# The last 64 columns of w_out loaded after the experts and unpacked as a ninth unit

## The chip, the cores and the metric

The kernel runs on one core of a Trainium2 chip. The metric is the device time of one execution in microseconds (us); shorter is better. A profiled execution also gives a trace, whose times count from the start of its span.

## The reference

Three layers run one after the other on 4608 tokens of 512 values:

```python
p_packed = sm_attn(p, k, v)              # attention into 32 packed rows, then back out
x = sm_attn(q, p_packed, p_packed)       # (batch 8, heads 8, 576, 64) -> (4608, 512)

logits = x @ phi                         # soft mixture of 8 experts, 4 slots each
slot_out[e] = relu(slot_input[e] @ w1[e]) @ w2[e]
x = softmax(logits, 1) @ slot_out

h = x @ w_in                             # 512 -> 1024
solu = h * softmax(h)
ln = (solu - mean) / sqrt(var + 1e-6) * g_ln
out = ln @ w_out                         # 1024 -> 512
```

[...]

## The kernel before

It has three phases. Phase 1 does the attention and the slots, unit by unit. Phase 2 streams the experts' weights (`w`, 29 loads of up to nine granules of 128x256) through TensorE, where a product per expert or block ends in `SO`. Then `sw` = `SO` x `wif` (the unpacked w_in) is summed over four pieces c for two halves n; the last, `sw(3, n)`, needs the last block's `SO`. `mk_sw` evicts each half on ACT and DVE into `swr`. Phase 3 makes 36 tiles of 128 tokens: `h` = cT x `swr` (`h_pe`), its negated row maximum (`nm`, `m_dve`), the exponential, `s3t`, the statistics on Pool, `hi` and `lo`, and the output matmuls `o` against `whi` and `wlo`, the two 16-bit halves of w_out.

All loads go out on SP's queue in the order of the list `order`, and land in 14 ring slots of 9216 bytes a partition (plus four in `ring2`). w_out is four loads of two chunks of 128x512 each, put in front of `("w", 4)` (`WO_AT`). They stay in their slots until the two halves have been made.

A w_out chunk is unpacked so (`mk_unpack`): DVE takes the exponent bits (`ux`, L1212) and the top mantissa word (`ua`, L1215), ACT scales the exponent by a Relu into bf16 bits (L1222), DVE adds the low word and the sign (L1227, L1234), and Pool multiplies both into the chunk (L1287). `wo_bound` lets TensorE add up |g| x exponents over all eight chunks into the bank `bd` (L1277). When all eight are in, ACT copies the bank to `winv` and DVE makes from it a power of two per column, `wsc`, and its inverse (L1296 to L1314). Then each chunk is scaled on DVE (`q1`, L1324), rounded on Pool to `whi` (`q2`, L1329), and the rest goes to `wlo` (`q3`, L1332).

The order of the work on each engine is fixed when the kernel is built. `Plan.op(engine, ns, function, deps, acq, rel, ...)` lists the operations with assumed durations, `LAT` holds assumed delays between engines, and `simulate` runs an engine's readiest and most urgent operation first: an engine that is free takes whatever is ready, and of several the one with the greatest `way` (longest way to the end, plus `urgent`). A random search with a fixed seed then shifts priorities and keeps what shortens the goals; phases 1 and 2 share one plan, phase 3 has its own, and all of the first plan stands ahead of the second on every engine. An engine executes in that order and waits wherever an input is late. Phase 3's tiles (`ep`, `tp`, `s3`) are laid over the ring's memory; one that lies over a ring slot waits until that slot's tile is released.

Of the kernel before, what the change touches and what calls it, by code (L numbers as in the profile page):

```python
# [185 lines left out]
def pack_attention__soft_moe__solu_kernel(  # L186
# [43 lines left out]
    WO_AT = 4  # L230
    NS1, NS2, NS3 = 122, 125, 142
# [21 lines left out]
    with ExitStack() as p12, tc.manual_schedule():  # L253
# [90 lines left out]
        for key in order:  # L344
# [13 lines left out]
            else:  # L358
                ns = 2540 if key[0] in ("wo", "wi") else 2850
# [835 lines left out]
        def mk_unpack(key, c, tail, deps, between=None):  # L1195
            def words():
                raw = loaded[key][:, 1024 * c:1024 * c + 1024].bitcast(UINT32).rearrange("p (n w) -> p n w", w=2)
                return raw[:, :, 0], raw[:, :, 1]

            def top():  # L1200
                raw = loaded[key][:, 1024 * c:1024 * c + 1024].bitcast(UINT16).rearrange("p (n w) -> p n w", w=4)
                return raw[:, :, 3]

            def dve():
# [3 lines left out]
                else:  # L1208
                    a = W["k"].tile([128, 512], FP32, tag="ua", name="ua")
                ua_t[key, c] = a  # L1210
                x = ux_t[key, c] = uk.tile([128, 512], UINT16, tag="ux", name="ux")
# [27 lines left out]
            ns = (1130, 670, 610, 740) if so else (1100, 720, 740, 1000)  # L1239
# [17 lines left out]
        def wo_chunk(k):  # L1257
            return loaded["wo", k // 2][:, 1024 * (k % 2):1024 * (k % 2) + 512]
# [14 lines left out]
        def wo_bound(k, key, c, dep):  # L1273
            def pe():
                if k == 0:
                    ps_t["bd"] = bank2()
                nc.tensor.matmul(  # L1277
                    out=ps_t["bd"], lhsT=W["ga"][:, k, :], rhs=ux_t[key, c].bitcast(BF16), start=(k == 0), stop=(k == 7)
                )

# [14 lines left out]
        def sc_act():  # L1295
            nc.scalar.copy(W["inv"], ps_t.pop("bd"))  # L1296

        def sc_dve():
            b = W["inv"].bitcast(UINT32)
            nc.vector.tensor_scalar(out=b, in0=b, scalar1=0x7F800000, scalar2=None, op0=ALU.bitwise_and)  # L1300

        def sc_dve2():
            W["sc"] = W["k"].tile([128, 512], FP32, tag="ua", name="wsc")
            nc.vector.tensor_scalar(
                out=W["sc"], in0=W["inv"].bitcast(UINT32), scalar1=24.0 * 2.0 ** 23, scalar2=None, op0=ALU.max
            )
# [476 lines left out]
```

## Time and profile before

| | us |
|---|---|
| median of three runs | 399.04 (398.42 to 399.07) |
| profiled execution | 398.32 |
| its span | 396.5 |

The profile shows for each engine when it worked and what ended its waits: PE is TensorE's matmul (PEld its weight loads), DVE VectorE, ACT ScalarE, POOL GpSimd, SP the queue that issues the loads. Busy time is given for the span and for stretches of it; the chain of waits goes back from the last instruction to what released each step. A wait for several things is put down to the one that came last.

### The profile page before, as it was taken

The page shows a single profiled execution, that of the slowest core. Times are in us where ns is not written, and L with a number is a line of the kernel's source. Part 1 is how long each engine was busy: PE and PEld are TensorE (multiplying, and loading weights), DVE is VectorE, ACT ScalarE, POOL GpSimd, SP SyncE. Part 2 cuts the span into 40 slices and gives each one's busy share as a digit, 9 for nine tenths or more (in the row PEclk, how much of TensorE's full clock was granted, in tenths as well). Part 3 has the DMA queues.
Part 4 walks back from the last instruction along what each step waited for, and adds up shares of the span by engine and source line. Part 5 has one row for each costly group of instructions (what it writes and reads, how often), then busy time and mean ns, then how long its engine had stood idle before and what let it go on. Part 6 is the DMA issues. An engine that isn't in the chain of part 4 may idle for free.

```text
span 396.5 us, 9563 instructions
## 1 busy us (share of the span) xinstructions
PE 375.6 (95%) x3760; PEld 198.0 (50%) x3760; DVE 285.4 (72%) x563; ACT 232.6 (59%) x437; POOL 205.9 (52%) x314
## 2 busy tenths in 40 slices
PE   8888999988989999798999999999999999999996
PEld 3456566656535664553444444444444444444445
DVE  2168899997977889917997766776677667766721
ACT  1447787887644654116978665666566656665610
POOL 1032456263234556892769665556555655565540
PEclk9999999998999999999999999999999999999999
DMA  8999999999999999940367956685776766756761
GB/s 308 423 419 416 418 419 415 419 418 414 421 416 421 421 414 422 416 189 1 62 128 157 185 122 145 136 158 120 147 157 135 122 145 156 138 119 145 140 152 54
DMA packets 89420, 99.25 MB, mean 250 GB/s; under 512 B 75936, under 2 KB 76576, under 8 KB 82080
## 3 DMA queue, kind: packets, MB, share of 16 engines
q1 hardware_dynamic: 89088, 98.58, 77.1%
q8 instruction: 29, 0.48, 0.5%
q14 instruction: 15, 0.12, 0.1%
q10 hardware_dynamic: 288, 0.07, 0.1%
HBM read 70.85 MB, written 9.44 MB: 202 GB/s over the span
## 4 chain that ended last, share of the span: by engine, by line
PE 62%; DMA 17%; DVE 13%; ACT 3%; issue 1%; POOL 1%; SPq 1%; DVEq 0%; ACTq 0%; POOLq 0%
PE o L1592 30%; PE o L1598 15%; DMA r<-w 8%; DMA r<-kT 6%; PE h L1416 3%; DMA r<-qT 3%; PE w L1039 3%; DVE bsum L603 2%; DVE bmx L583 2%; PE sc L411 1%; PE o L1605 1%; DVE nm L1424 1%; DVE nb L431 1%; PE sw L1350 1%; ACT a L436 1%
## 5 line engine op out<-in xcount | busy, mean ns | idle before, releaser
L1592 PE MATMUL o<-whi,th 128*128 128x512 f16 x280 | 106.1, 379 | 0.6 <-DVE nm L1424 0.5
L1592 PE MATMUL o<-wlo,th 128*128 128x512 f16 x280 | 106.1, 379 | 0.0
L1565 POOL TENSOR_TENSOR lo<-x,hi 128x1024 f16<-128x1024 f32 (+1 forms) x37 | 77.2, 2089 | 53.0 <-issue 47.1
L1592 PEld LDWEIGHTS <-th 128*128 128x128 f16 x560 | 54.5, 98 | 66.6 <-DMA th<-hi 1.5
L1440 ACT ACTIVATE e<-h,nm 128x1024 f32<-128x1024 f32 (+1 forms) x37 | 40.3, 1090 | 50.5 <-DVE nm L1424 50.5
L1598 PE MATMUL o<-whi,tl 128*128 128x512 f16 x280 | 66.5, 380 | 0.0
L1424 DVE TENSOR_REDUCE nm<-h 128x1 f32<-128x1024 f32 (+1 forms) x37 | 43.9, 1193 | 28.2 <-PE h L1416 28.2
L1497 ACT ACTIVATE e<-s3t,nv 128x1024 f32<-128x1024 f32 x35 | 40.2, 1147 | 10.9 <-DVE nmean L1462 10.9
L1543 ACT ACTIVATE hi<-s3t,nr,rs 128x1024 f16<-128x1024 f32 x35 | 43.4, 1240 | 5.1 <-POOL nr L1526 5.0
L1450 DVE SCALAR_TENSOR_TENSOR s3t<-h,e 128x1024 f32<-128x1024 f32 (+1 forms) x36 | 43.5, 1207 | 1.8
L1620 DVE TENSOR_TENSOR ob<-o,winv 128x512 f32<-128x512 f32 x35 | 24.2, 691 | 25.3 <-PE o L1598 25.3
L1598 PEld LDWEIGHTS <-tl 128*128 128x128 f16 x280 | 25.0, 98 | 34.0 <-issue 7.7
L1535 DVE TENSOR_SCALAR x<-s3t,nmean,rs 128x1024 f32<-128x1024 f32 x35 | 30.7, 877 | 0.4 <-POOL rs L1522 0.4
L1416 PE MATMUL h<-swr,cT 96*128 96x512 f32 x72 | 28.8, 483 | 1.2 <-DVE swr L1362 0.9
L469 POOL TENSOR_SCALAR r<-s 128x1 f32<-128x1 f32 x16 | 4.4, 274 | 39.7 <-ACT a L436 39.6
L395 PE MATMUL w<-wz 128*128 128x512 f16 x83 | 22.9, 379 | 0.5 <-DVE A L590 0.4
L1522 POOL TENSOR_TENSOR rs<-rs,half 128x1 f32<-128x1 f32 x36 | 20.2, 560 | 2.8
L1039 PE MATMUL w<-r,SIT 128*32 128x256 f32 x256 | 21.5, 383 | 0.0
L436 ACT ACTIVATE a<-sc,nb 128x576 f32<-128x576 f32 x16 | 11.8, 739 | 13.8 <-DVE nb L431 13.5
L431 DVE TENSOR_REDUCE nb<-sc 128x1 f32<-128x576 f32 x16 | 11.6, 753 | 10.4 <-PE sc L411 10.2
L1416 PEld LDWEIGHTS h<-swr,cT 96*128 96x128 f32 x72 | 13.6, 190 | 7.6 <-issue 1.5
L1287 POOL TENSOR_TENSOR r<-ua,ux 128x512 f32<-128x512 f32 x8 | 10.6, 1335 | 12.6 <-DMA r<-w 4.5
(227 smaller groups left out, 644.6 us busy)
## 6 DMA issues: line engine op xcount, KB each, us to landing
r<-w SPq DMA_DIRECT2D x27, 1152.0 KB, 17.5
r<-v SPq DMA_DIRECT2D x8, 1152.0 KB, 21.1
r<-kT SPq DMA_DIRECT2D x7, 1152.0 KB, 22.1
r<-qT SPq DMA_DIRECT2D x7, 1152.0 KB, 22.0
out<-ob SPq DMA_DIRECT2D x31, 256.0 KB, 2.3
r<-w_in SPq DMA_DIRECT2D x4, 1024.0 KB, 21.9
r<-w_out SPq DMA_DIRECT2D x4, 1024.0 KB, 21.6
r<-w SPq DMA_DIRECT2D x3, 512.0 KB, 17.0
```

The source lines that it names most:

```text
L1039: nc.tensor.matmul(out=hp[32 * g:32 * g + 32, 0:256], lhsT=SIT[:, k, :], rhs=gran(i), start=(k == 0), stop=(k == 3),)
L1416: nc.tensor.matmul(out=w, lhsT=cT[t % 4][:, t // 4, :], rhs=swr[n], start=True, stop=True)
L1424: nc.vector.tensor_reduce(out=z["nm"][:, h:h + 1], in_=hcols(h), axis=AX.X, op=ALU.max, negate=True)
L1440: nc.scalar.activation(out=z["e"][:, cols(h)], in_=hcols(h), func=ACTF.Exp, bias=z["nm2"] if h else z["nm"][:, 0:1], accum_out=z["S"][:, h ...
L1450: nc.vector.scalar_tensor_tensor(out=z["s"][:, cols(h)], in0=hcols(h), scalar=z["f"] if H == 2 and h == 0 else 1.0, in1=z["e"][:, cols(h)] ...
L1497: nc.scalar.activation(out=z["e"], in_=z["s"], func=ACTF.Square, bias=z["nv"], scale=2.0 ** -15, accum_out=z["V"])
L1535: nc.vector.tensor_scalar(out=z["x"][:, cols(h)], in0=z["s"][:, cols(h)], scalar1=z["n"], scalar2=z["r"], op0=ALU.add, op1=ALU.mult,)
L1543: nc.scalar.activation(out=z["hi"][:, cols(h)], in_=z["s"][:, cols(h)], func=ACTF.Identity, scale=z["r"], bias=z["nr"])
L1565: nc.gpsimd.tensor_tensor(out=z["lo"][:, cols(h)], in0=z["x"][:, cols(h)], in1=z["hi"][:, cols(h)], op=ALU.subtract)
L1592: nc.tensor.matmul(out=z["o"], lhsT=z["th"][:, c, :], rhs=w[:, c, :], start=(c == 0 and w is whi), stop=False)
L1598: nc.tensor.matmul(out=z["o"], lhsT=z["tl"][:, c, :], rhs=whi[:, c, :], start=False, stop=(c == 7))
L1620: nc.vector.tensor_tensor(out=z["ob"], in0=z["o"], in1=winv, op=ALU.mult)
```

## The change

w_out is stored as two parts. The first 448 columns (`WM`) are loaded and unpacked where all 512 were, as chunks of 128x448. The last 64 (`WL`) of all eight chunks, 512 numbers a partition, make a fifth load, which goes out after the experts' last one, and a ninth unit for `mk_unpack`. For it there are eight bound matmuls of 64 columns in a bank of their own, a second `mk_sc` on 64 columns, eight 64-column multiplies on DVE that make the scale times g (`last_scale`), and on Pool the scaling product, `hi` and `lo`. The scratch of these steps is the rest of the ninth unit's own ring slot. The plan's assumed durations follow the sizes, and phase 3's plan has one empty Pool operation of 3000 ns at its start.

```diff
+    WM, WL = 448, 64
...
             order.append(("w", i))
+        order.append(("wo", 4))
...
-                    src = (w_out if key[0] == "wo" else w_in)[key[1]].bitcast(UINT32)
-                    nc.sync.dma_start(out=t[:, :2048].bitcast(UINT32), in_=src)
+                    if key[0] == "wi":
+                        src = w_in[key[1]]
+                    else:
+                        src = w_out[:, 2 * WM * key[1]:2 * WM * key[1] + (2 * WM if key[1] < 4 else 8 * WL)]
+                    src = src.bitcast(UINT32)
+                    nc.sync.dma_start(out=t[:, :src.shape[1]].bitcast(UINT32), in_=src)
...
-                ns = 2540 if key[0] in ("wo", "wi") else 2850
+                ns = {"wi": 2540, "wo": 2540 * WM // 512, "v": 2850}[key[0]]
+                if key == ("wo", 4):
+                    ns = 2540 * WL // 128
                 ld[key] = op("DMA", ns, load(key, 0), acq=[ring_of(key)], lat=2200)
...
+            N = 512 if key[0] == "wi" else WM if key[1] < 4 else 8 * WL
...
-            ns = (1130, 670, 610, 740) if so else (1100, 720, 740, 1000)
+            ns = (1130, 670, 610, 740) if so else (980, 660, 660, 890)
+            if key == ("wo", 4):
+                ns = (820, 720, 690, 690)
             x = op("DVE", ns[0], dve, deps, acq=["u", "x"], soft=so)
             y = op("ACT", ns[1], act, [x], soft=so)
...
+            def pe_last():
+                ps_t["bd"] = bank2()
+                x = ux_t[key, c].bitcast(BF16)
+                for j in range(8):
+                    nc.tensor.matmul(
+                        out=ps_t["bd"][:, :WL], lhsT=W["ga"][:, j, :], rhs=x[:, WL * j:WL * j + WL], start=(j == 0), stop=(j == 7)
+                    )
+
+            if k == 8:
+                o_bd.append(op("PE", 320, pe_last, [dep, o_bd[-1]], acq=["v"], rel=["x"], pairs=8))
+                return o_bd[-1]
...
+        x = mk_sc("sc", slice(0, WM), o_bd[-1], 390, ["u"], lambda: W["k"].tile([128, 512], FP32, tag="ua", name="wsc")[:, :WM])
...
-                nc.gpsimd.tensor_copy(W["hi"][:, k, :], wo_chunk(k))
+                nc.gpsimd.tensor_copy(W["hi"][:, k, :WM], wo_chunk(k))
...
+        def last_scale(js):
+            t = loaded["wo", 4]
+            g, s = t[:, 1536:1536 + 8 * WL], t[:, 2176:2176 + WL]
+            for j in js:
+                nc.vector.tensor_scalar(
+                    out=g[:, WL * j:WL * j + WL], in0=s, scalar1=g_sb[:, j:j + 1], scalar2=None, op0=ALU.mult
+                )
+
+        def last_q1():
+            t = loaded["wo", 4]
+            nc.gpsimd.tensor_tensor(
+                out=t[:, 1024:1024 + 8 * WL], in0=wo_chunk(8), in1=t[:, 1536:1536 + 8 * WL], op=ALU.mult
+            )
+
+        def last_src():
+            return loaded["wo", 4][:, 1024:1024 + 8 * WL].rearrange("p (k n) -> p k n", k=8)
+
+        def last_q2():
+            nc.gpsimd.tensor_copy(W["hi"][:, :, WM:], last_src())
+
+        def last_q3():
+            nc.gpsimd.tensor_tensor(out=W["lo"][:, :, WM:], in0=last_src(), in1=W["hi"][:, :, WM:], op=ALU.subtract)
+
+        o_l = mk_unpack(("wo", 4), 0, wo_tail, [ld["wo", 4], o_2], wo_bound)
+        x = mk_sc("sc2", slice(WM, 512), o_bd[-1], 110, [], lambda: loaded["wo", 4][:, 2176:2176 + WL])
+        x = [op("DVE", 400, lambda j=j: last_scale(range(j, j + 4)), [x]) for j in (0, 4)]
+        x = op("Pool", 1330, last_q1, [*x, o_l])
+        x = op("Pool", 820, last_q2, [x, o_3])
+        o_last = op("Pool", 1310, last_q3, [x])
...
         o_sw = op("DVE", 700, lambda: None, urgent=10 ** 6)
+        op("Pool", 3000, lambda: None, urgent=10 ** 6)
```

`mk_sc` holds the five steps that made `wsc` before (one copy on ACT, four operations on DVE), now for a range of columns.

## Rows read from the trace of the kernel before

**Rows 1.** The page's head: span, and busy time of TensorE's two rows and the others.
```profile
span 396.5 us, 9563 instructions
...
PE 375.6 (95%) x3760; PEld 198.0 (50%) x3760; DVE 285.4 (72%) x563; ACT 232.6 (59%) x437; POOL 205.9 (52%) x314
```

**Rows 2.** Stretches: length, busy us (instructions) per engine, clock, DMA share, GB/s.
```profile
165.00:170.00 5.00, 4.64 (x76) 2.96 (x78) 4.74 (x4) 0.69 (x3) 5.00 (x5) 1.00 1.00 411
170.00:175.00 5.00, 4.68 (x82) 2.60 (x78) 0.00 (x0) 0.48 (x2) 5.00 (x7) 1.00 0.62 244
...
200.00:210.00 10.00, 9.40 (x43) 4.46 (x42) 9.43 (x12) 7.41 (x12) 7.58 (x13) 1.00 0.71 133
...
260.00:300.00 40.00, 40.00 (x185) 18.74 (x184) 28.93 (x50) 25.56 (x36) 24.13 (x44) 1.00 0.69 141
```

**Rows 3.** Chain of waits: start us, us, what.
```profile
141.31 16.49 DMA r<-w
157.81 16.96 DMA r<-w
```

**Rows 4.** Expert load line L321, 160 to 162 us: the last load.
```profile
L321 SPq DMA_DIRECT2D r<-w x1: 328/328/328, 160.7 to 160.7; - x1
...
DMA to landing us min/median/max: 15.4/15.4/15.4
```

**Rows 5.** Instructions in time: start, us, engine, line, operation, [idle before <-releaser].
```profile
178.25 0.21 ACT L1074 ACTIVATE SO<-w 128x48 f32<-128x48 f32 x1 [0.81 <-PE w L1147]
178.51 1.96 PE L1350 MATMUL sw<-wif,SO 128*96 128x512 f32 x4 [0.30 <-ACT SO L1074]
180.26 0.69 DVE L1362 TENSOR_TENSOR swr<-sw,swr 32x512 fp32r<-32x512 f32 x1 [10.53 <-ACT swr L1358]
181.12 0.69 DVE L1362 TENSOR_TENSOR swr<-sw,swr 32x512 fp32r<-32x512 f32 x1 [0.17 <-ACT swr L1358]
181.84 1.29 DVE L1424 TENSOR_REDUCE nm<-h 128x1 f32<-128x512 f32 x2
```

**Rows 6.** Same view: steps of the last units, and transposes as nearest to narrow matmuls.
```profile
143.61 1.39 DVE L1212 TENSOR_SCALAR ux<-r 128x512 uint16<-128x512 uint16 x1 [1.40 <-PE v L1277]
...
153.57 0.41 DVE L1212 TENSOR_SCALAR ux<-r 128x512 uint16<-128x512 uint16 x1
...
154.08 0.72 ACT L1222 ACTIVATE ux<-ux,ebias 128x512 uint16<-128x512 uint16 x1 [1.26 <-DVE ux L1212]
155.27 0.59 ACT L1296 COPY winv<-v 128x512 f32<-128x512 f32 x1 [0.47 <-PE v L1277]
...
189.85 0.38 PE L1579 MATMUL tr<-ident,hi 128*128 128x128 f16 x4 [0.37 <-DVE th L1583]
```

**Rows 7.** Narrow DVE operations: three in time, and line L505 (ns min/median/max).
```profile
123.10 0.16 DVE L930 RECIPROCAL rf<-rf 128x1 f32<-128x1 f32 x1
123.30 0.16 DVE L931 TENSOR_TENSOR rf<-rf,df 128x1 f32<-128x1 f32 x1
...
187.41 0.15 DVE L1459 TENSOR_SCALAR nv<-ms 128x1 f32<-128x1 f32 x1
187.48 0.14 DVE L1462 TENSOR_SCALAR nmean<-ms 128x1 f32<-128x1 f32 x1
...
L505 DVE TENSOR_SCALAR pb<-w,r x16: 260/276/290, 13.3 to 98.8; 128x64 f32<-128x64 f32 x16
```

**Rows 8.** In time: Pool's first and last pass, and first steps of phase 3.
```profile
161.56 0.91 POOL L1329 CAST whi<-r 128x512 f16<-128x512 f32 x1 [1.83 <-DVE r L1324]
...
176.29 0.61 POOL L1329 CAST whi<-r 128x512 f16<-128x512 f32 x1
176.98 1.16 POOL L1332 TENSOR_TENSOR wlo<-r,whi 128x512 f16<-128x512 f32 x1
...
184.38 0.74 DVE L1450 SCALAR_TENSOR_TENSOR s3t<-h,f,e 128x512 f32<-128x512 f32 x1
184.43 0.34 POOL L1505 TENSOR_SCALAR S<-S,f 128x1 f32<-128x1 f32 x1 [6.29 <-ACT e L1440]
```

More of the change, by code (lines that the diff above doesn't have):

```diff
@@ L1208, in dve @@
                 else:
[L1209 removed]
+                    a = W["k"].tile([128, 512], FP32, tag="ua", name="ua")[:, :N]
                 ua_t[key, c] = a
[L1211 removed]
+                x = ux_t[key, c] = uk.tile([128, 512], UINT16, tag="ux", name="ux")[:, :N]
                 nc.vector.tensor_scalar(
@@ L1308, in sc_dve3, with mk_sc, sc_act, sc_dve @@
-        def sc_dve3():
-            nc.vector.tensor_scalar(
-                out=W["inv"].bitcast(UINT32), in0=W["sc"], scalar1=-23.0 * 2.0 ** 23, scalar2=None, op0=ALU.add
-            )
-        def sc_dve4():
-            nc.vector.tensor_scalar(
-                out=W["sc"].bitcast(UINT32), in0=W["sc"], scalar1=-1.0, scalar2=267.0 * 2.0 ** 23,
-                op0=ALU.mult, op1=ALU.add,
-            )
-        x = op("ACT", 480, sc_act, [o_bd[-1]], rel=["v"])
-        for f in (sc_dve, sc_dve2, sc_dve3, sc_dve4):
-            x = op("DVE", 430, f, [x], acq=["u"] if f is sc_dve2 else [])
+        def mk_sc(name, cols, dep, ns, acq, tile_of):
+            inv, z = W_inv(cols), {}
+            def sc_act():
+                nc.scalar.copy(inv(), ps_t.pop("bd")[:, 0:cols.stop - cols.start])
+            def sc_dve():
+                b = inv().bitcast(UINT32)
+                nc.vector.tensor_scalar(out=b, in0=b, scalar1=0x7F800000, scalar2=None, op0=ALU.bitwise_and)
+            def sc_dve2():
+                z["sc"] = W[name] = tile_of()
+                nc.vector.tensor_scalar(
+                    out=z["sc"], in0=inv().bitcast(UINT32), scalar1=24.0 * 2.0 ** 23, scalar2=None, op0=ALU.max
+                )
+            def sc_dve3():
+                nc.vector.tensor_scalar(
+                    out=inv().bitcast(UINT32), in0=z["sc"], scalar1=-23.0 * 2.0 ** 23, scalar2=None, op0=ALU.add
+                )
+            def sc_dve4():
+                nc.vector.tensor_scalar(
+                    out=z["sc"].bitcast(UINT32), in0=z["sc"], scalar1=-1.0, scalar2=267.0 * 2.0 ** 23,
+                    op0=ALU.mult, op1=ALU.add,
+                )
+            x = op("ACT", 100 + ns, sc_act, [dep], rel=["v"])
+            for f in (sc_dve, sc_dve2, sc_dve3, sc_dve4):
+                x = op("DVE", ns, f, [x], acq=acq if f is sc_dve2 else [])
+            return x
@@ L1758, in _layout @@
         "w_in": _words(x["moe2_w_in"]).reshape(4, 128, 1024),
-        "w_out": _words(x["moe2_w_out"]).reshape(4, 2, 128, 512).transpose(0, 2, 1, 3).reshape(4, 128, 1024),
+        "w_out": np.concatenate(
+            [a.transpose(1, 0, 2).reshape(128, -1) for a in np.split(_words(x["moe2_w_out"]).reshape(8, 128, 512), [448], axis=2)], axis=1
+        ),
         "g_ln": x["moe2_g_ln"].reshape(8, 128).transpose(1, 0),
```

29 lines of the change are left out of this document (12 added, 17 removed).

## The prediction

> **What bounds the kernel now.** I read the page's totals first [rows 1]: TensorE is busy for 375.6 us of a span of 396.5 us. That average hides two stages, which the table of stretches separates [rows 2]. Up to about 170 us the DMA engines move 411 GB/s at a share of 1.00; from 170 to 175 us it falls to 244 GB/s, as the last load drains. From 260 to 300 us TensorE is busy for 40.00 of 40.00 us. So the first stage lasts as long as its loads and the last stage as long as its matmuls, and what lies between is a chain.
>
> The chain of waits [rows 3] runs through two DMA pieces, the second from 157.81 to 174.77 us. The very last load, granules 252 to 255 of the experts, is issued at 160.7 us and lands 15.4 us later, at 176.05 us [rows 4] (160.65 where the time of issue is shown to two digits). Behind it stand the last expert block, the sum `SO`, the last two `sw` products, their evictions, and phase 3's first reduction `nm` at 181.84 us [rows 5]. What ends the load stage earlier moves this chain earlier, unless new work gets into it.
>
> **The gain.** The four early pieces of w_out shrink from 512 to 448 columns, by 64 x 1024 x 8 B = 524 kB in all; at the 411 to 418 GB/s of a saturated stretch (411 in [rows 2]) that is 1.25 to 1.28 us, and the last landing lies 176.05 - 174.77 = 1.28 us behind the one before, for 524 kB as well [rows 3, 4]. I take 1.25. All expert loads land that much earlier, the last at 174.8. The bytes come back behind them, so the ninth unit lands where the last load landed before: 176.05. SP queues nothing between it and phase 3's first transpose; its slot in the ring is long free, and 12 us of transfers are queued ahead of it, so issuing it costs nothing; were that cover gone, it would be late by the time of issue.
>
> [...]
>
> The chain moved by 1.25 us would give `SO` at 177.0, the `sw` pair at 177.26, DVE's two `swr` at 179.0 and 179.87, and `nm` at 180.59 [rows 5].
>
> **What the ninth unit adds to that chain.** Its steps are all on engines that the chain uses, in a program order fixed beforehand. Where the order of the plan decides, I laid out the planner's rule by hand with the costs in the diff; that settles an order, not a time of the chip. The planner thinks that the unit lands 0.57 us after the last expert load (1270 - 700 ns); then the Relu is ready on ACT 47 ns before the last `SO`, the bound matmuls are ready on PE some 0.23 us before `sw(3,0)`, and both go first. DVE then has: four narrow `sc2` steps, half of `last_scale`, `swr0`, the other half, `swr1`. On the chip the unit lands 1.25 us after the expert load, so engines wait for it in that order.
>
> Step by step, on the clock of the trace: landing 176.05; `ux` 0.41 with Pool idle [rows 6] and about 0.05 for each hand-over, 176.5; Relu 0.72, 177.3; the bound's eight matmuls of 64 columns start 0.05 later. Nearest row: four 128-column transposes in 0.38, of which one is 0.22, so 0.055 a pair; eight take 0.6, to 177.95 [rows 6]. Their issue holds PE until 177.8, so `sw(3,0)` starts there and not at 177.26: 0.55 late. That alone takes under half of the gain.
>
> The longer delay is DVE's. ACT copies the 64 columns in 0.2 (512 take 0.59 [rows 6]), to 178.2. Then DVE has four dependent steps on 64 columns: 0.20 apart on one column, where each needs the one before [rows 7]; I take 0.22, 0.9 in all. Eight independent multiplies of 64 columns: between 0.07 from start to start (two single-column ones at 187.41 and 187.48) and 0.28 (128x64 from PSUM, whole duration) [rows 7]; I take 0.13, nearer the first, as the 0.28 includes a pipeline that overlaps; 1.05 in all. Two `swr` of 0.69 that overlap a little, 1.3 [rows 5]. From 178.2 that ends at 181.45, and `nm` starts there: 0.85 to 0.9 after the 180.59 of the moved chain. DVE was idle for ten microseconds ahead of `swr0` before, so this load is hidden only up to the time of its own last input.
>
> Pool: the two passes over w_hi and w_lo were busy from 161.56 to 178.14; with 448 columns they take 7/8, and DVE's unpacking ahead of them also 7/8, so they end by about 174 and are out of the unit's way. The unit's own Pool work begins with its product at 178.3 (1.2, hidden) and then q1, q2 and q3 after the second half of `last_scale` (about 180.8): 1.16 + 0.61 + 1.16 with DVE idle and hand-overs, 3.2 in all [rows 8], to 184.0; up to 3.7 where DVE's operations get between. Pool's first work of phase 3 stood at 184.43 before [rows 8], 2.6 after `nm`; it would be 184.05 now. So Pool is just about ready.
>
> One more wait is new. Phase 3's tiles lie over the closed ring. In the layout of the kernel before, the tile that the rotation would give next, the slot of `("w", 19)`, lies under `s3t` of tile 0, which DVE writes 2.54 us after `nm` [rows 5, 8]; now it may be written only after Pool's last q3. 181.45 + 2.54 = 184.0 against 184.0 to 184.5: a wait of 0 to 0.5, behind which all of DVE stands in order; I put it at 0.1 as the slot may be another.
>
> **Sum.** 1.25 - 0.9 - 0.1 = 0.25 us gained. The first o matmul moves by that, and the matmul-bound stage behind it keeps its length; TensorE's 9.40 of 10.00 us at 200 to 210 [rows 2] is the only slack there, 0.6 us. The profiled execution had 398.32 us around its span of 396.5, and would have 398.07; it stands 0.72 below the median of 399.04, on which I forecast 398.8. Bounds: the narrow DVE work at 0.07 a multiply and 0.20 a dependent step gives 0.55 + 0.8 and `nm` at 180.9, a gain of 0.95 (398.1); at 0.20 a multiply, 0.25 a step, 0.1 a bound pair and 0.5 of the slot wait, `nm` is near 182.3 and the gain -0.95 (400.0). 0.2%, about what a measurement of this kernel can tell from no change, is 0.8 us, so the forecast lies inside it.
>
> **Rivals.** (a) *All of it hidden*: the chain keeps the whole 1.25 us, 397.8. For it: DVE was idle for 10.5 us up to 180.26. Against it: the last input of its new work can't be there before 178.2. (b) *Late bound, slower*: the bound matmuls are put behind the two last `sw`, which issue until 179.2. Then `sc2` starts on DVE only at 180.1 and `nm` behind 1.95 us of narrow steps at 182.05, 1.45 late; Pool ends at 185.3, and where the slot lies under `s3t` (ready at 184.6) 0.7 more is lost: 1.25 - 2.15 = -0.9, 399.9, to 400.3 with the dearer steps. It decides from 0.23 us of the plan's arithmetic. (c) *Pool still busy at the landing*: `ux` then takes 1.39 and not 0.41, as at 143.61 while Pool ran [rows 6]; everything behind is 1.0 later, -0.75, 399.8. For it: Pool had work until 178.14 before. Against it: the 7/8 above. (d) *Slot under phase 3's small tiles*: then `nm` itself waits for Pool's end near 184: 3.4 us late, 2.2 slower, 401.2. One of ten rotating slots. (e) *Not what it says*: the random search of both plans is drawn anew, and another order of DMA waits or of phase 3's first tiles moves the end by half a microsecond either way or stalls a load; it adds width rather than a case.
>
> The Trainium skill, SBUF — State Buffer, section on the two separate sides, calls the port that VectorE and GpSimd share an exclusive lock, held for a whole instruction. The rows agree: 0.41 against 1.39 for the same instruction [rows 6]. By that rule rival (c) gives its 399.8.
>
> **How the numbers follow.** Forecast 0.56 (398.1 to 400.0), (a) 0.14, (b) 0.15, (c) 0.07, (d) 0.08. Faster than 398.24: (a) and the best fifth of the forecast, 0.26. Slower than 399.84: (b) and (d), half of (c) and little of the forecast, 0.26. The same: 0.48. The range 397.7 to 400.3 holds the forecast, (a), (c) and most of (b), and leaves out (d).
>
> **What would show it.** Right: last expert landing near 174.8 and the ninth unit near 176.05; the bound matmuls between the last `SO` and `sw(3,0)`; DVE without a gap from about 178.2 to `nm` near 181.5; the first o matmul at about 189.8 (before 190.07). Wrong: a gap on DVE ahead of `nm` (then the chain is PE's or (a) holds), the bound behind `sw` (b), `ux` over 1 us (c), `s3t` or `nm` released by Pool (slot), or DMA below 410 GB/s ahead of 170 us (e).

## The result, and the profile after

The changed kernel took 404.62 us (404.28 to 405.85), the kernel before 399.06 beside it (398.42 to 399.48): a ratio of 1.0143, 95% interval 1.0118 to 1.0168. The forecast was 398.8, with a range up to 400.3: wrong, and by 1.4%. The profiled execution took 405.85 around a span of 403.9, 7.5 more than that of the kernel before; positions in the two traces differ by up to that, while the medians differ by 5.56. (This profile is of the slowest of the four executions.)

The page's head of the kernel after (span; busy time, share and instructions of each engine) answers to [rows 1]:

```profile
span 403.9 us, 9607 instructions
...
PE 378.9 (94%) x3769; PEld 197.5 (49%) x3769; DVE 290.6 (72%) x579; ACT 232.4 (58%) x439; POOL 207.1 (51%) x318
```

The totals hardly moved, so I went to the two places that [rows 2] had separated. First the load stage. Stretches of the kernel after, with length, busy us (instructions) of PE, PEld, DVE, ACT and POOL, granted clock, DMA share and GB/s:

```profile
128.00:130.00 2.00, 1.93 (x40) 1.20 (x40) 1.42 (x6) 0.72 (x3) 1.62 (x2) 1.00 0.88 359
130.00:132.00 2.00, 1.88 (x19) 1.30 (x22) 0.81 (x5) 1.25 (x2) 0.60 (x1) 1.00 0.50 207
132.00:134.00 2.00, 2.00 (x37) 0.98 (x25) 2.00 (x5) 1.05 (x2) 0.53 (x1) 1.00 0.07 22
134.00:136.00 2.00, 2.00 (x24) 0.86 (x23) 2.00 (x3) 0.68 (x2) 0.00 (x0) 1.00 0.92 295
```

The same stretch of the kernel before:

```profile
130.00:132.00 2.00, 2.00 (x20) 0.74 (x16) 2.00 (x3) 1.77 (x4) 0.00 (x0) 1.00 1.03 418
132.00:134.00 2.00, 2.00 (x46) 1.40 (x47) 1.85 (x4) 1.81 (x3) 0.88 (x1) 1.00 0.98 410
```

The loads ran dry: 22 GB/s for two microseconds. Over the four stretches, (59 + 211 + 396 + 123) x 2 / 418 = 3.8 us of transfers at 418 GB/s are missing. What SP's queue waited for between 84 and 170 us (total, times, longest, in us) says why:

```profile
SPq L323 <- PE w L1047: 25.6, 6, 18.4
```

and in the kernel before:

```profile
SPq L321 <- PE w L1039: 16.7, 4, 12.0
```

L1047 (L1039 before) is the experts' first matmul, which frees ring slots. It started at 131.62 and not at 126.05: the search over the first plan had found another order, which on the chip ends phase 1 5.6 us later. (From the first o matmul on, the instructions of PE, DVE, ACT and Pool come in the same order in both traces, so phase 3's order is not among the suspects.) All slots were full, and the queue stood.

The last expert load, L323, and the ninth unit's, L330 (issue, and time to landing), answer to [rows 4]:

```profile
L323 SPq DMA_DIRECT2D r<-w x1: 327/327/327, 163.0 to 163.0; - x1
...
DMA to landing us min/median/max: 15.3/15.3/15.3
```

```profile
L330 SPq DMA_DIRECT2D r<-w_out x1: 328/328/328, 165.8 to 165.8; - x1
...
DMA to landing us min/median/max: 13.8/13.8/13.8
```

They landed at 178.3 and 179.5; before, the last one landed at 176.05. Moving 1.27 us of bytes behind should have given 174.8, and 3.8 us of missing transfers make 178.6 of that: the stall is enough to account for the landing.

Then the chain behind the landing. DVE in time (start, us, line, operation, [idle before <-releaser]); the last two `swr` and `nm` answer to [rows 5]:

```profile
179.62 0.43 DVE L1222 TENSOR_SCALAR ux<-r 128x512 uint16<-128x512 uint16 x1 [7.39 <-DMA r<-w_out]
179.96 1.36 DVE L1225 TENSOR_SCALAR ua<-r 128x512 uint32<-128x512 uint32 x1
...
182.70 0.19 DVE L1327 TENSOR_SCALAR winv<-winv 128x64 uint32<-128x64 uint32 x1
183.33 0.97 DVE L1331 TENSOR_SCALAR r<-winv 128x64 f32<-128x64 uint32 x1 [0.44 <-PE sw L1413]
...
184.79 0.74 DVE L1375 TENSOR_SCALAR r<-r,g_sb 128x64 f32<-128x64 f32 x4
185.56 0.69 DVE L1425 TENSOR_TENSOR swr<-sw,swr 32x512 fp32r<-32x512 f32 x1
186.28 0.74 DVE L1375 TENSOR_SCALAR r<-r,g_sb 128x64 f32<-128x64 f32 x4
187.06 0.69 DVE L1425 TENSOR_TENSOR swr<-sw,swr 32x512 fp32r<-32x512 f32 x1
187.78 1.41 DVE L1488 TENSOR_REDUCE nm<-h 128x1 f32<-128x512 f32 x2
189.22 1.14 DVE L1494 TENSOR_TENSOR nm<-nm 128x1 f32<-128x1 f32 x1
```

Pool in the same stretch:

```profile
179.69 1.36 POOL L1189 CAST cT<-chi 32x1152 fp32r<-32x1152 f32 x1
183.10 1.15 POOL L1311 TENSOR_TENSOR r<-ua,ux 128x512 f32<-128x512 f32 x1 [2.05 <-PE sw L1413]
...
189.19 1.15 POOL L1392 TENSOR_TENSOR wlo<-r,whi 128x512 f16<-128x512 f32 x1
```

Lay the two lists over each other: three DVE instructions take about a microsecond instead of 0.42, 0.20 and 0.16, and beside each of them one Pool instruction runs. `nm` starts at 187.78, 5.94 later than before, though the last `sw` pair (181.15) is only 2.64 later.

TensorE in time:

```profile
180.92 0.39 PE L1297 MATMUL v<-ux,ga 128*128 128x64 bf16 x8 [0.46 <-ACT ux L1232]
181.15 1.94 PE L1413 MATMUL sw<-wif,SO 128*96 128x512 f32 x4
186.40 0.47 PE L1480 MATMUL h<-swr,cT 96*128 96x512 f32 x1 [3.32 <-DVE swr L1425]
187.80 1.51 PE L1480 MATMUL h<-swr,cT 96*128 96x512 f32 x3 [0.93 <-DVE swr L1425]
189.11 3.47 PE L1774 MATMUL fill<-wz 128*128 128x512 f16 x10
...
197.09 0.38 PE L1656 MATMUL o<-whi,th 128*128 128x512 f16 x1
```

The first o matmul is 7.02 later than before (190.07). From there to the end of the last one it is 203.16 us before and 203.60 after: that stage kept its length but for 0.44, nearly as predicted. TensorE stood idle for 3.32 us ahead of `h`, and the clock granted from 188 to 191 us was 0.50, the lower of its two levels (1.2 of 2.4 GHz); before, it was 1.00 from 181 to 190. The ten fill matmuls (products of a zero tile that compute nothing) took 3.47 where they took 2.33 before. In this execution that cost next to nothing: the chain of waits goes from `nm`'s second stage (189.22) to the next `nm` (190.28) and through none of the fill matmuls. `nm` to the first o took 9.31, against 8.23 before, and the second stage's 1.14 instead of 0.16 is 0.98 of that 1.08.

So three suspects: the order of phase 1, the ninth unit's work on the chain, and the clock.

### The profile page after: what moved, and what is told of

The parts are those of the page before. It is cut to its first block, busy times and chain, and to the rows that moved or that the text cites. A ratio compares the mean times of both kernels' runs of the same rounds, so it can differ in the third digit from the quotient of the medians.

```text
span 403.9 us, 9607 instructions
## 1 busy us (share of the span) xinstructions
PE 378.9 (94%) x3769; PEld 197.5 (49%) x3769; DVE 290.6 (72%) x579; ACT 232.4 (58%) x439; POOL 207.1 (51%) x318
## 4 chain that ended last, share of the span: by engine, by line
PE 61%; DMA 18%; DVE 12%; ACT 5%; issue 2%; POOL 1%; ACTq 0%; DVEq 0%; POOLq 0%; SPq 0%
PE o L1656 29%; PE o L1662 14%; DMA r<-kT 9%; DMA r<-w_out 3%; PE h L1480 3%; PE w L1047 3%; DMA r<-w 3%; PE sc L419 2%; PE w L1098 1%; PE o L1669 1%; DVE bmx L591 1%; PE w L693 1%; DMA g_sb<-g_ln 1%; DVE wif L1225 1%; DMA th<-hi 1%
## 5 line engine op out<-in xcount | busy, mean ns | idle before, releaser
L1599 DVE TENSOR_SCALAR x<-s3t,nmean,rs 128x1024 f32<-128x1024 f32 x35 | 32.3, 923 | 0.2 <-POOL rs L1586 0.2
L403 PE MATMUL w<-wz 128*128 128x512 f16 x84 | 24.6, 380 | 1.2 <-ACT bq L530 0.5
L1047 PE MATMUL w<-r,SIT 128*32 128x256 f32 x256 | 22.5, 384 | 0.0
L1222 DVE TENSOR_SCALAR ux<-r 128x512 uint16<-128x512 uint16 (+1 forms) x17 | 11.5, 675 | 10.2 <-DMA r<-w_out 7.4
```

The source lines that it names most:

```text
L403: nc.tensor.matmul(out=t[:, 0:FN], lhsT=wz[:, 0:128], rhs=wz[:, 0:FN], start=True, stop=True)
L1047: nc.tensor.matmul(out=hp[32 * g:32 * g + 32, 0:256], lhsT=SIT[:, k, :], rhs=gran(i), start=(k == 0), stop=(k == 3),)
L1599: nc.vector.tensor_scalar(out=z["x"][:, cols(h)], in0=z["s"][:, cols(h)], scalar1=z["n"], scalar2=z["r"], op0=ALU.add, op1=ALU.mult,)
```

## The experiments

Medians; where not said otherwise ten executions each, compared with the kernel before on the same chip (398.62 to 399.17). A trace is of one execution and can lie away from the median: it took 401.50 in e1 (median 400.64), 401.03 in e2 (399.75), 400.44 in e11 (399.80) and 397.18 in e3 (397.57), so distances between these traces can be larger than those between the medians.

### The order of phase 1, and the unit

`e1_old_order`: the changed kernel; the first plan, which holds phases 1 and 2, gets the priorities that the search had found for the kernel before, and isn't searched. Its order of phase 1 is then that of the kernel before, on every engine. Phase 3's plan gets its own priorities back, which are the same for both kernels.

```diff
-        best, order = way, self.simulate(way, True)
-        low = self.worth(order)
+        if self.given:
+            way = [w if g is None else g for w, g in zip(way, self.given)]
+            self.goals = []
+        best, order = way, [] if self.given else self.simulate(way, True)
+        low = 0 if self.given else self.worth(order)
...
+        plan.given = GIVEN1
...
+        plan.given = GIVEN3
```

> The changed kernel, with the priorities that the search had found for the kernel before given to the first plan (the new operations keep their plain ones), so that phase 1 runs in exactly the order of the kernel before. Theory A (the order of phase 1, drawn anew, ends phase 1 at 131.7 instead of 126.1 us, the ring stays full, the queue runs dry and the last load lands 3.5 us later): phase 1 ends near 126, the load rate has no dip at 130 to 134 us, the last expert load lands near 174.8 and the ninth unit near 176.05; what is left is the ninth unit's tail of 3.3 + 1.1 + 0.4 us against the 1.25 gained: 401 us (400.5 to 402.5). Theory B (the dip comes from the loads themselves, the 7168-byte rows or the fifth load's slot): the dip stays, 404 to 405 us.

Measured: 400.64, ratio 1.0039 (1.0021 to 1.0057). Theory A held: 3.98 of the 5.56 are gone, or 3.60 where each kernel is set against the kernel before that was measured beside it (+5.56 and +1.96). The loads don't stall (419 GB/s from 132 to 134), the last expert load lands at 175.2.

`e2_new_order_in_before`: the kernel before with the order that the changed kernel had found, by the same edit.

> The kernel before, unchanged but for the priorities of its first plan, which are those that the search found for the changed kernel; phase 1 runs in exactly the changed kernel's order. Theory A: phase 1 ends near 131.7, the load rate dips near 132 us, the last load lands about 3.5 us later than 176.05 and the time is 399.1 + 3.5 = 402.5 us (401.5 to 403.5). Theory B: no dip, 399 us.

Measured: 399.75, ratio 1.0012 (0.9990 to 1.0034), profile span 398.9. Theory A's stall came, its time did not: 1.07 above the kernel before, not 3.5. The loads fall to 179 GB/s from 132 to 134, the last one lands at 178.0 and `nm` is at 184.20, and nothing else is late. That is one half of a useful fact: with this order the last expert load lands at 178.0 in the kernel before and at 178.3 in the changed one. Taking 524 kB out of the early loads brought nothing: from 130 to 136 us the loads ran at 327, 179 and 212 GB/s here and at 207, 22 and 295 there, so the queue ran dry earlier and waited for the same slots.

`e3_old_order_no_unit`: as e1, the ninth unit's load stays and its instructions are left out; the last 64 columns of w_out and of their scale are constants, so 64 columns of the output are not computed.

```diff
+            if key == ("wo", 4):
+                dve = act = dve2 = dve3 = lambda: None
...
+            if name == "sc2":
+                sc_act = sc_dve = sc_dve2 = sc_dve3 = sc_dve4 = lambda: None
```

> As the changed kernel with the old order of phase 1, the fifth load still made, but none of the ninth unit's instructions issued (the last 64 columns of w_out are blank, so of the output's last 64 columns nothing is computed); the plan keeps their places. If the load's move is worth its bytes and the tail's loss is all the ninth unit's: last expert load at 174.8, first reduction nm near 180.6, first output matmul near 188.8, 399.1 - 1.25 = 397.8 us (397.4 to 398.3). If moving the load is worth nothing by itself: 399 us.

Measured: 397.57, ratio 0.9968 (0.9952 to 0.9983). The gain of the move alone is real, 1.11 us. Last expert load at 159.6 + 15.4 = 175.0; DVE:

```profile
180.81 1.29 DVE L1626 TENSOR_REDUCE nm<-h 128x1 f32<-128x512 f32 x2
```

`nm` is 1.03 earlier than in [rows 5], 0.22 behind the 180.59 at which the prediction had put the moved chain.

`e11_new_order_no_unit`: the fourth cell, the changed kernel's own order with the same instructions left out.

> The changed kernel with its own order (404.62), with the ninth unit's load but without its instructions; the last 64 columns of w_out and their scale are set to constants on Pool, so the last 64 columns of the output are not computed. It completes a table of two orders, with and without the unit: old order 397.57 without and 400.64 with it. Theory A (the new order costs by its later last load, the unit adds its own delay on top and meets Pool's late cast): the last expert load lands near 178.3, 3.2 later than with the old order, nm near 183.9, and the time is 397.57 + 3.2 = 400.8, or down to 399.6 as the same order cost the kernel before only 1.1; the unit then costs 3.8 to 5.0 in this order, against 3.07. Rival (the new order costs the same 3.98 whether the unit is there or not): 401.4 or more, and the unit again 3.1.

Measured: 399.80, ratio 1.0012 (0.9995 to 1.0030); last expert load at 162.7 + 15.3 = 178.0, and

```profile
183.82 1.29 DVE L1679 TENSOR_REDUCE nm<-h 128x1 f32<-128x512 f32 x2
```

3.01 behind e3, as the load is. Theory A held; by the medians, each against the kernel before beside it, the order costs 1.74. The four cells, as differences from the kernel before that was measured beside each:

| | without the unit | with the unit |
|---|---|---|
| old order of phase 1 | -1.11 | +1.96 |
| new order of phase 1 | +0.63 | +5.56 |

Load moved: -1.11. Unit's work: +3.07. New order: +1.74. What the last two cost only together: 5.56 + 1.11 - 3.07 - 1.74 = +1.86. With intervals of 0.6 to 1.0 either way in the cells, that last term is the least sure (about 1.5 either way, an estimate from the four intervals). The trace of the changed kernel shows 0.94 that fits it: in the new order Pool's cT cast was still to come and fell on the unit's `ua` (1.36, and 0.42 in e1). That this is the whole of it isn't shown.

### What the unit costs

All of these have the old order, so they compare with e1. Its DVE and Pool:

```profile
178.99 0.20 DVE L1459 TENSOR_SCALAR r<-winv 128x64 f32<-128x64 uint32 x1
179.22 1.03 DVE L1464 TENSOR_SCALAR winv<-r 128x64 uint32<-128x64 f32 x1
180.28 0.20 DVE L1469 TENSOR_SCALAR r<-r 128x64 uint32<-128x64 f32 x1
...
183.50 0.69 DVE L1617 TENSOR_REDUCE nm<-h 128x1 f32<-128x512 f32 x1
...
185.09 0.99 DVE L1623 TENSOR_TENSOR nm<-nm 128x1 f32<-128x1 f32 x1
```

```profile
179.01 1.19 POOL L1439 TENSOR_TENSOR r<-ua,ux 128x512 f32<-128x512 f32 x1 [2.32 <-DVE winv L1455]
```

`e5_no_unit_pool`: Pool does nothing for the unit.

```diff
-            return op("Pool", 1330, pool, z, rel=["u"])
+            return op("Pool", 1330, pool if key[1] < 4 else lambda: None, z, rel=["u"])
...
-        x = op("Pool", 1330, last_q1, [*x, o_l])
+        x = op("Pool", 1330, lambda: None, [*x, o_l])
```

> As e1_old_order, but Pool does nothing for the ninth unit: its product, scaling, hi and lo are left out and the last 64 columns of both halves of w_out are zeroed earlier, so the last 64 columns of the output are not computed. DVE's work for the unit is all there. Theory P (two of DVE's narrow steps wait for Pool, not for their inputs): the step of 1.03 goes back to 0.20 and nm2 from 0.99 to 0.16; nm at 182.7, the two gains add to 1.66, and the time is 400.64 - 1.66 = 399.0 (398.6 to 399.4). Rival (the two steps are long for another reason, as a late scalar or the form of the instruction): both stay near 1.0 and the time stays at 400.3 to 400.7.

Measured: 399.86, ratio 1.0022 (1.0009 to 1.0035). The two rows did what theory P says:

```profile
179.61 0.20 DVE L1464 TENSOR_SCALAR winv<-r 128x64 uint32<-128x64 f32 x1
...
184.38 0.16 DVE L1626 TENSOR_TENSOR nm<-nm 128x1 f32<-128x1 f32 x1
```

That Pool held them up is shown. The time fell by 0.78 and not by 1.66, between the two theories. In the profiled execution a main pass of Pool's ran beside `ux` (0.86, not 0.43), and its 400.08 stand 2.8 around the span of 397.3, where the other profiled ones have 1.7 to 2.1. Why the time fell by no more stays open.

`e4_scale_off_dve`: `last_scale` goes; Pool multiplies by g and by the scale, each broadcast.

```diff
-        x = [op("DVE", 400, lambda j=j: last_scale(range(j, j + 4)), [x]) for j in (0, 4)]
-        x = op("Pool", 1330, last_q1, [*x, o_l])
+        o_g4 = op("Pool", 1330, last_g, [o_l])
+        x = op("Pool", 1330, last_q1, [x, o_g4])
```

> The changed kernel with the old order of phase 1 (as e1_old_order, 400.64), and the eight 64-column multiplies of last_scale taken off DVE: Pool multiplies the chunks by g, broadcast along the columns, and then by the scale, broadcast along the chunks. Theory T (the ninth unit costs what its DVE work puts between the last sum and nm): DVE loses two groups of 0.74, nm comes 1.46 earlier than 183.50, at 182.0, and the time is 400.64 - 1.46 = 399.2, a little less if TensorE's shorter gap keeps its clock up: 398.7 to 399.6. Rival P (DVE's steps are long because Pool works beside them, whatever their number): the third narrow step stays near 1.0, and with one more Pool product beside DVE another step or an eviction is held up by about 0.8; nm at 182.8 or later, 400.0 to 400.6.

Measured: 399.41, ratio 1.0011 (0.9992 to 1.0030). Time as by T, row as by P: `nm` at 182.99 and not at 182.0, because with two Pool products in a row the fourth narrow step also took 1.08. Of the 1.48 that DVE no longer does, the fourth step takes back 0.88.

`e6_fills_keep_clock`: ten fill matmuls in TensorE's gap.

```diff
         plan.run()
+        fill = bank()
+        for _ in range(10):
+            nc.tensor.matmul(out=fill, lhsT=wz[:, 0:128], rhs=wz, start=True, stop=True)
```

> As e1_old_order, with ten more 512-column matmuls on a zero tile put on TensorE behind the last sw, where it was idle from 180.04 to 182.12. Nothing of the computation changes. Theory C (the idle time costs TensorE its clock, granted 0.50 from 184 to 190): the clock is granted 1.00 there, the ten fill matmuls before phase 3's first tile take 2.3 and not 4.49, and the first o comes 1 to 2 earlier than 193.69; time 398.9 to 399.9. Rival (the lower clock lies under waits for the other engines and costs nothing): clock 1.00 but first o within 0.3 of 193.69 and the time within 0.3 of 400.64.

Measured: 399.59, ratio 1.0011 (1.0001 to 1.0020): 1.05 less than e1. TensorE of e1, then of e6:

```profile
182.12 0.47 PE L1609 MATMUL h<-swr,cT 96*128 96x512 f32 x1 [2.08 <-DVE swr L1553]
...
184.98 4.49 PE L1903 MATMUL fill<-wz 128*128 128x512 f16 x10
```

```profile
182.34 0.47 PE L1612 MATMUL h<-swr,cT 96*128 96x512 f32 x1
...
184.37 2.34 PE L1906 MATMUL fill<-wz 128*128 128x512 f16 x10
```

And the stretch from 186 to 188 (the sixth figure is the granted clock), e1 and then e6:

```profile
186.00:188.00 2.00, 2.00 (x7) 0.60 (x5) 1.97 (x6) 1.66 (x4) 0.72 (x4) 0.50 0.00 0
```

```profile
186.00:188.00 2.00, 1.74 (x9) 0.70 (x7) 1.93 (x8) 1.78 (x5) 1.23 (x6) 1.00 0.00 0
```

Theory C held. In e1 the chain of waits itself (start, us, what) runs through the slow fill matmuls:

```profile
185.18 4.29 PE fill L1903 x10
```

Ten instructions that compute nothing became the path once the clock had fallen. `nm` is no earlier in e6 (183.54), the first o is, by 1.89 in these two traces. More than the fills changed, though: with `h` at the full clock `nm`'s second stage came ahead of Pool's `wlo` in e6, and so took 0.16 and not 0.99:

```profile
184.86 0.16 DVE L1626 TENSOR_TENSOR nm<-nm 128x1 f32<-128x1 f32 x1
...
184.96 1.16 POOL L1520 TENSOR_TENSOR wlo<-r,whi 128x512 f16<-128x512 f32 x1
```

So the 1.05 is the price of the lower clock with what followed from it, and isn't to be added to that of the second stage.

`e7_unit_rebuilt`: e4, Pool's product put behind the narrow steps in the plan, and nm's second stage as a reduction with one input.

```diff
-                nc.vector.tensor_tensor(out=z["nm2"], in0=z["nm"][:, 0:1], in1=z["nm"][:, 1:2], op=ALU.min)
+                nc.vector.tensor_reduce(out=z["nm2"], in_=z["nm"], axis=AX.X, op=ALU.min)
```

> All that the ninth unit seems to cost, mended: as e4_scale_off_dve, with Pool's product only behind DVE's narrow steps, and nm2 as a reduction over one tile of two columns and not as an operation on two inputs. By theories T and P together: narrow steps 0.2 each, nm near 181.3, nm2 0.2, no long gap on TensorE; the kernel without the unit's instructions took 397.57, and four narrow steps of 0.2 with the bound's 0.55 add 0.7 to 1.0: 398.3 to 398.6, which would be level with the kernel before (398.7). Rival (Pool now ends later, near 185.5, and phase 3's first tiles wait for it): 399.3 or more.

Measured: 399.04, ratio 0.9998 (0.9985 to 1.0010), level with the kernel before, and between the times of the two sides. The reduction took 0.16 beside Pool's wlo; the narrow steps still took 1.03 and 1.08. A place behind them in the plan is no wait: Pool had nothing else to do, so its product started when its own inputs were there, at 178.92.

`e8_pool_behind_scale`: Pool's first operation is now g times scale, which needs the last narrow step's result, and the rest follows.

```diff
+        x = op("Pool", 1330, last_gs, [x])
+        o_l = op("Pool", 1330, pool, [*z, x], rel=["u"])
+        x = op("Pool", 1330, last_q1, [o_l])
```

> As e7_unit_rebuilt (399.04), but Pool now really starts behind DVE's four narrow steps: its first operation makes g times the scale, which needs the last of them; the unit's product, the scaling, hi and lo follow. In e7 Pool's product started 0.25 us after DVE's first narrow step ended, and the third and fourth took 1.03 and 1.08. Theory P (they were held up by Pool): all four take 0.2, DVE is done by 179.2, ahead of ACT's half of swr at about 179.7, so swr and nm wait for TensorE's eight bound matmuls alone: nm at 181.3 and not 182.64, no long gap on TensorE, and the time is 399.04 - 1.3 = 397.7 (397.4 to 398.2), faster than the kernel before. Rival (Pool's end matters as well: five operations from 179.2 end near 184.6, and phase 3's first statistics or tile wait for it): 398.5 or more.

Measured: 398.43, ratio 0.9993 (0.9972 to 1.0014). Half of each. DVE did as theory P says, and then came the wait that the rival named:

```profile
179.18 0.20 DVE L1472 TENSOR_SCALAR r<-r 128x64 uint32<-128x64 f32 x1
...
181.14 1.29 DVE L1624 TENSOR_REDUCE nm<-h 128x1 f32<-128x512 f32 x2
...
184.95 0.75 DVE L1650 SCALAR_TENSOR_TENSOR s3t<-h,f,e 128x512 f32<-128x512 f32 x1 [1.20 <-POOL wlo L1525]
```

`nm` came at 181.14 (181.3 expected), and `s3t` waited 1.20 for Pool's last operation: in this kernel the unit's ring slot lies under the first tiles' `e` and `s3t`.

`e9_tile_off_the_slot` allocated two more `s` tiles first. They were never used and were given away again, so tile 0's `s3t` had the same place; it is a second run of e8.

> As e8_pool_behind_scale (398.43), with phase 3's s3t rotation started two buffers later, so that tile 0's s3t doesn't lie over the unit's slot of the ring. In e8 nm came at 181.14, but s3t waited 1.20 for Pool's wlo until 184.9. Theory S (that slot's wait was what ate e8's gain): s3t of tile 0 at 183.7, the first o between 189.0 and 189.8 (190.50 in e8), time 397.2 to 397.9, faster than the kernel before. Rival (Pool's five operations themselves hold up phase 3's first statistics, which are Pool's too): s3t at 183.7 but Pool's first statistics still at 184.9 and the first o within 0.3 of 190.5; 398.2 to 398.6.

Measured: 398.73, ratio 1.0012 (0.9990 to 1.0034), the same wait of 1.20. The expectation wasn't tested.

`e10_slot_under_x`: e8 with `x` and `lo` laid out ahead of `e` and `s`, which takes `e` and `s3t` off the slot.

```diff
+        ep.tile([128, 1024], FP32, tag="x", name="x_first")
+        ep.tile([128, 1024], FP16, tag="lo", name="lo_first")
```

> As e8_pool_behind_scale (398.43), with phase 3's big tiles laid out in another order: x and lo first, so that x and lo and not e and s3t lie over the unit's ring slot. (e9 changed nothing: its two extra tiles were never used, the rotation gave tile 0 the same place, and s3t waited 1.20 for Pool's wlo again.) Theory S (that slot's wait ate part of e8's gain): s3t of tile 0 follows nm without the wait of 1.20, near 183.7 for a landing as in e8; Pool's first statistics still stand behind its wlo, at about 184.9, and take half of it back; the first o 0.5 to 1.1 earlier relative to the unit's ux than in e8 (14.19), and 397.4 to 398.0. Rival (Pool's work is the bound): first o within 0.3 of e8's distance, 398.2 to 398.7.

Measured: 398.56, ratio 1.0010 (0.9983 to 1.0037):

```profile
184.53 0.74 DVE L1652 SCALAR_TENSOR_TENSOR s3t<-h,f,e 128x512 f32<-128x512 f32 x1
...
189.37 1.19 DVE L1753 TENSOR_SCALAR hi<-s3t,nmean,rs 128x256 f16<-128x256 f32 x3 [1.66 <-POOL rs L1724]
```

The slot's wait is gone and another stands in its place: phase 3's first statistics are Pool's too, they start behind its wlo (185.77), and `hi` waits 1.66 for them (0.78 in the kernel before, 0.70 in e8). By its time the rival held: the unit's five Pool operations, 5.4 us from the last narrow step, take most of the gain back. By the distance from `ux` to the first o neither side did: it is 14.68, 0.49 more than in e8, but in this execution Pool's last main pass also ran beside `ux` (1.25, not 0.43), and without those 0.82 it would be 0.33 less.

### Does the change force the late order?

Other seeds of the random search, nothing else, in both kernels:

```diff
-        rnd = random.Random(1)
+        rnd = random.Random(2)
```

> The kernel before with another seed of the random search in both plans; nothing else. Theory A (a new draw of the order of phase 1 costs or gives microseconds by itself): the time differs from 398.9 by over 0.8 in at least one of the two new draws of this kernel, most likely upward (399 to 403), in step with the time at which phase 1's last operations let the ring's slots go (stretches of 2 us ahead of 140 below 300 GB/s). Rival (the order was bad in the changed kernel because of what the change puts into the plan): both new draws of the kernel before stay within 0.8 of 398.9.

> As before_draw2 with a third seed; the same expectations hold for the two together.

> The changed kernel with another seed of the random search in both plans; nothing else. Theory A (most of what was lost, 3.98 of 5.56, is the draw): another draw moves the time by over 1 from 404.6, to between 399.7 (the lowest of the changed kernel with the old order) and 403.5. Rival (the change itself drives the plan to this order, as by its later last load): 404 to 405.5 again, with the same fall of the load rate at 130 to 134.

> The changed kernel with a fourth seed of the random search. Of six seeds, in the plan's own time, phase 1 ends between 123.6 and 125.3 in the kernel before and between 124.1 and 127.0 in the changed one; this seed is the 124.1, the first one stood at 125.6 (404.6 on the chip), the second at 127.0 (406.2). Theory A' (the order that the search happens to find sets the time, and the changed kernel can have an early one): no fall of the load rate ahead of 140, the last expert load lands at 175 to 176.3, time 400.2 to 402.0, as with the old order (400.64). Rival (the change forces the loads to stall, whatever the order): last landing at 178 or later, 403.5 or more.

> The changed kernel with a third seed of the random search. So far its draws took 404.6, 406.2 and 408.3, those of the kernel before 398.7, 399.7 and 398.6, and the changed kernel with the order of the kernel before 400.64. Theory F (the changed plan leads the search to orders that the chip runs badly): this and after_draw5 are 403 or more. Theory L (luck of the draw): at least one of the two comes to 402 or less.

> As after_draw3, with a fifth seed; the same expectations hold for the two together.

> The kernel before with the fourth seed, which gave the changed kernel its 408.3. Theory F: 400 or less, like the other draws of this kernel. Theory L (draws of either kernel spread over several us): as likely above 401 as below it.

Measured (the changed kernel's draws four executions each), with the start of the experts' first matmul and the lowest load rate in a stretch of 2 us from 130 to 138 us:

| order | experts' start | lowest GB/s | median (range) |
|---|---|---|---|
| before, draw 1 | 126.05 | 410 | 399.06 (398.42 to 399.48) |
| before, draw 2 | 128.37 | 354 | 399.73 (398.85 to 404.45) |
| before, draw 3 | 128.21 | 340 | 398.63 (397.84 to 399.82) |
| before, draw 4 | 126.98 | 406 | 398.77 (398.33 to 399.31) |
| after, draw 1 | 131.62 | 22 | 404.62 (404.28 to 405.85) |
| after, draw 2 | 129.67 | 216 | 406.24 (404.12 to 408.56) |
| after, draw 3 | 126.74 | 395 | 403.56 (400.35 to 407.62) |
| after, draw 4 | 134.96 | 51 | 408.26 (406.45 to 409.88) |
| after, draw 5 | 132.02 | 36 | 406.53 (405.45 to 410.39) |
| after, old order (e1) | 126.22 | 400 | 400.64 (399.73 to 401.50) |

Theory A of before_draw2 (a redraw by itself costs or gives microseconds) held by its letter and not in its size: draw 2 lies 0.83 above 398.9, at a ratio of 1.0052 (1.0013 to 1.0091), the other two new draws of the kernel before are level with it, and no median is at 401 or more. But three of draw 2's ten executions took 403.56, 403.81 and 404.45, like the changed kernel's draws; the profile is of an execution of 398.99 and doesn't say why. Neither side of after_draw2 named its 406.24. Theory A' of after_draw4 fell too, and badly: 408.26 where 400.2 to 402.0 was expected. Theory F held by the medians: all five of the changed kernel lie at 403.6 to 408.3, and draw 4 of the kernel before at 398.77. For draw 3 that says little: its four executions took 400.35, 402.09, 405.02 and 407.62. It isn't forced, since e1 is the changed kernel as well; draw 3, too, shows in its profile (of the 400.35) an early phase 1 and no stall, and why its other executions took up to 407.62 that profile can't say. One stretch of the changed kernel's draw 4, whose plan had the earliest end of phase 1 of its six:

```profile
134.00:136.00 2.00, 2.00 (x28) 1.19 (x31) 1.39 (x2) 0.67 (x1) 1.14 (x2) 1.00 0.12 51
```

In the plan's own time phase 1 ended at 124.1 there; on the chip the experts started at 134.96. The assumed durations don't rank these orders as the chip does. The traces show two ways in which the draws lose: the stall (draws 1, 4 and 5), and Pool's main passes still running at the unit's landing (draw 2: until 182.24, with `ux` to the narrow steps at 0.43, 0.78, 1.41, 0.93, 1.02, 0.54, 1.08; draws 4 and 5 have this as well). The second costs the kernel before nothing: its draw 2 has Pool busy until 181.24 and takes 399.73. What in the changed plan led the search to late or crowded orders in four draws, and to one that is unsteady in the fifth, was not found.

## Why the prediction was wrong, point by point

Two steps failed. The larger is rival (e), the order drawn anew, which got no chance and no price. The other is the sum for the unit on the chain: with the old order kept it gives 400.64 (e1), already above the range's 400.3.

- **What bounds the kernel**: right. Load stage, chain, matmul stage; the last was 0.44 us longer (203.60, 203.16).
- **The gain of 1.25**: right as a mechanism where the loads don't stall, and a little large: last landing at 175.0 instead of 174.8, 1.11 us of time (e3). In the order that the search found for the changed kernel it was nothing (last landing at 178.0 without the move in e2, 178.3 with it and 178.0 in e11).
- **Rival (e), "it adds width rather than a case"**: the step that failed first. The prediction saw that the search is drawn anew and that a load might stall, and then gave it half a microsecond either way and no chance. It cost 1.74 alone and 3.60 together with what it does to the unit, against the unit's own 3.07. Its sign, loads below 410 GB/s ahead of 170 us, came (22). The trace of before shows what hangs on the order, though not the price: SP's queue waits there for the experts' first matmuls for 16.7 us in all, longest 12.0. The loads live from slots that phase 1's end sets free, and an order that ends phase 1 by 5.6 later empties the queue, as e2 shows in the kernel before itself. The 411 GB/s of [rows 2] holds in the changed kernel too (418 from 165 to 170 us); that the loads never stand still before it was an effect of the order, and was used as if it were a property of the stage.
- **Ninth unit 1.25 behind the last load**: right, 1.26 (178.27 and 179.53) and 1.25 in e1 (175.23 and 176.48); no row shows a price of that load beyond its bytes.
- **Bound between `SO` and `sw(3,0)`**: right (180.77, 180.92, 181.15), and `sw(3,0)` came 0.62 later than without the unit (178.10 in e1, 177.48 in e3). Of that 0.23 is the last expert load, which landed that much later in e1's trace (175.23, 175.00), so 0.39 is the bound's, against 0.55 predicted; its eight matmuls took 0.39 and not 0.6.
- **Four narrow steps of 0.22, 0.9 in all**: three took 0.19 to 0.20, one 0.97 to 1.03. This is the second step that failed, and its term is Pool's product, "1.2, hidden": it is hidden as a Pool operation and holds up a DVE step for most of its length. e5 and e8 show it from two sides. The prediction applied the shared port, of which SBUF — State Buffer of the Trainium skill (section on the two separate sides) says that with some DVE instructions one holder locks out the other for a whole instruction, to `ux` alone, in rival (c), and didn't walk it through the unit's other pairs.
- **Eight multiplies of 0.13, 1.05 in all**: mis-sized; 1.48 (0.74 for four).
- **`nm`**: at 183.50 in the old order, 2.05 later than the 181.45 of the sum: 0.83 from Pool's product, 0.43 from the multiplies, 0.53 from the unit's `ux` at 176.58 and not at 176.05, and 0.26 in hand-overs.
- **From `nm` to the first o**: taken as unchanged. Two things were missed, and one of the two ended last: in the changed kernel's trace nm's second stage beside Pool's wlo (1.14, not 0.16), in e1's the clock with the slow fills (1.05 us by e6). The prediction had `sw` and `nm` late and didn't ask what TensorE's longer idle time does.
- **Pool's main passes end by about 174**: wrong: 176.7 in e1, just as the unit landed, and 179.6 in the changed kernel. Where such a pass reached a little further over the landing, `ux` took 0.86 (e5) and 1.25 (e10): rival (c), decided by some tenths of a microsecond.
- **Slot under `s3t`, 0.1**: in the changed kernel the slot lies under `x` and `lo` and cost nothing; in e8 it lies under `e` and `s3t` and cost the 1.20. The mechanism is right, the place is drawn with the order.
- **Rivals**: (a) is e3's time (397.57 against 397.8), reached only without the unit; that e1's 400.64 lies just above (b)'s 400.3 is chance, since in e1 the bound stood ahead of `sw`.

Of the versions tried none that computes everything beats the kernel before: e4, e7, e8, e9 and e10 are level with it (ratios 0.9993 to 1.0012, all intervals with 1 in them). The 1.1 us of the move and the unit's cost cancel even when the order is kept and the unit is rebuilt.

## What to carry to other kernels

Where the order of the work is searched when the kernel is built, a change to any part redraws all of it: hold the old order (give the search's priorities) to price an edit, and give the redraw a case of its own, looking at who waits longest for slots. New work on an engine isn't hidden because that engine was idle: list what runs on DVE beside every Pool instruction, and what TensorE's longer gap does to its clock. Where the load queue stood still for want of slots, fewer early bytes did not land the last byte earlier (178.0 and 178.3).

## What was unexpected of the hardware

- A narrow DVE instruction can pay the full price of a Pool neighbour: 0.20 became 1.03 on 64 columns and 0.16 became 0.99 to 1.14 on a single column, beside Pool operations of 1.15 to 1.19. In e7 the same single-column step as a reduction with one input took 0.16 beside Pool's wlo; as an operation on two inputs it took 0.99 (e1). In e1 the second `swr` and the first half of `nm`, which take TensorE's sums as input, kept their 0.69 beside Pool's scaling product (182.90 to 184.16).
- An idle gap of 2.08 us on TensorE ahead of `h` was followed by a granted clock of 0.50 from 184 to 190 us (e1); in e4 and e7 the gap was 2.19 in both, the clock 0.50 from 182.5 to 185.5 in e4 and 1.00 throughout in e7. With the gap filled (e6) it stayed at 1.00.
